# Two-kind causal attention followed by a gated long convolution: the loads, casts and products of v one pair behind those of q and k, all engines in written order from the first instruction, masks built at their first use

## The chip, the cores and the metric

The kernel runs on one core of one Trainium2 chip. The metric is the device time in microseconds of one execution; the time of a kernel is the median of its runs. Before the change the three runs have a median of 232.93 us (232.51 to 232.97).

## The reference, cut to what matters

Inputs q, k and v have the shape (4 batches, 8 heads, 768 positions, 64). Heads 0, 2 and 6 attend to every earlier position; the others attend to the first 4 positions and to a window of 64. The heads' outputs, side by side, are the input x (4, 768, 512) of the second part, which is a projection, a circular convolution along the positions (here by real Fourier transforms), two gates and an output projection.

```python
scores = np.matmul(q, k.transpose(0, 1, 3, 2)) / np.sqrt(D)
mask = np.where(retrieval_head, causal, causal & (is_sink | in_window))
a = softmax(np.where(mask, scores, -1e9))
x = np.matmul(a, v).transpose(0, 2, 1, 3).reshape(B, S, H * D)
x1, x2, x3 = np.split(x @ w_proj, 3, axis=-1)
x2_conv = np.fft.irfft(np.fft.rfft(x2, axis=1) * np.fft.rfft(filter_fft, axis=0), n=S, axis=1)
out = (x1 * x2_conv * x3) @ w_out
```

## The kernel before, in words

The work is tiled into 16 pairs of heads, numbered n = 0 to 15: four batches of four pairs. A pair passes through these steps.

- `emit_loads` (L89): three loads on SP's queue, q and k into one tile `qk_f` and v into `v_f`, 384 KB each. Three buffers of each tile go round.
- `emit_cast` (L113): q and k to bf16, two casts on POOL (for pair 0, q is cast on ACT), into `qk_bf`.
- `emit_v` (L299), all on POOL: a memset of the ones column and a cast make `v_aug`; a product with `vmask` makes `v_far`, used for blocks of keys that lie two or more blocks back, where a windowed head sees only the first positions. Three buffers of `v_aug` go round, so pair n + 3 writes where pair n's values were read.
- `emit_prep` (L123): q and k transposed, head dimension to the partitions. For pairs 0 to 5 PE transposes 12 blocks into PSUM and ACT copies them to `qkT` (L137; for pair 0 DVE does, L135). From pair 6 on SP issues a transposing DMA (L139).
- `emit_chunks` (L308): the causal blocks of the scores, in six chunks (three "thirds"), PE to PSUM (L319), and ACT's exponential into `pT` (L326).
- `emit_masking` (L328): one DVE product per third with `mask` (L333). `emit_mask` (L232) builds one head's mask on DVE from `code` and the head's kind.
- `emit_values` (L335) and `emit_norm` (L351): PE's 42 products with `v_aug` and `v_far` (L344), then DVE's reciprocal `rec` (L354) and scaling into `attn` (L355).
- `emit_turn` (L358): `attn` transposed into the batch's `xT`, by PE with a DVE copy (L364) or by SP's transposing DMA (L366).

The main loop (L498) runs over the pairs. In round n it casts and values pair n + 2, loads pair n + 3, computes pair n's scores and pair n - 1's values. The second part of a batch (`moe`, L371) is a generator whose steps are put between the attention's steps (`gate_step`). `setup_steps` (L263) transforms the filter once, in rounds 3 to 5: its first PE product is `X_ps<-fold` (L255), which waits for DVE's `fold` (L266).

PSUM gives four tiles of two banks, taken in turn by everything that PE writes, so a late reader of one tile stops a later PE step. POOL also issues the weights' loads, which convert to bf16: `filt` (L488) in round 0, one third of `wproj` in round 2 and two thirds in round 3 (L492), `wout` in round 6.

What sets the order: each engine runs its instructions in one order. For POOL and SP that is the order written, throughout. For DVE it is the written one from L104 to round 5 (`MANUAL`), for PE and ACT from L468 to round 5; elsewhere a scheduler chose it. Before the main loop stand pair 0's steps, the constants of the Fourier matrix G (ACT's `turns`, DVE's `angle` and `size`, ACT's four Sin steps) and the masks' parts.

Of the kernel before, what the change touches and what calls it, by code (L numbers as in the profile page):

```python
# [9 lines left out]
FP32 = mybir.dt.float32  # L10
BF16 = mybir.dt.bfloat16
I32 = mybir.dt.int32
AF = mybir.ActivationFunctionType
# [31 lines left out]
def kernel(  # L45
# [13 lines left out]
    nc = tc.nc  # L59

    B, H, S, D = q.shape
    NT = S // 128
# [21 lines left out]
    state = {}  # L84
    pairs = [(b, hp) for b in range(B) for hp in range(HP)]
# [3 lines left out]
    def emit_loads(n):  # L89

        b, hp = pairs[n]
        qk = ald.tile([128, 2, 2, NT, D], FP32, name="qk_f32")
        vf = ald.tile([128, 2, NT, D], FP32, name="v_f32")
        rows = "h (p t) d -> p h t d" if n < BY_PE else "h (t p) d -> p h t d"
        for dst, src, order in ((qk[:, 0], q, rows), (qk[:, 1], k, rows), (vf, v, "h (t p) d -> p h t d")):
            nc.sync.dma_start(out=dst, in_=src[b, 2 * hp:2 * hp + 2].rearrange(order, p=128))
        return qk, vf

    BY_PE = 6
    MANUAL = 5  # L100
    engine = mybir.EngineType
    ctx.enter_context(tc.manual_schedule(engines={engine.Pool, engine.SP}))
    order = ExitStack()
    order.enter_context(tc.manual_schedule(engines={engine.DVE}))  # L104
    loads = {0: emit_loads(0)}
    ret_i64 = const.tile([128, H], mybir.dt.int64, name="ret_i64")
    nc.scalar.dma_start(out=ret_i64, in_=is_retrieval.partition_broadcast(128))


    def cast(out, in_):  # L110
        nc.gpsimd.tensor_copy(out=out, in_=in_)  # L111

    def emit_cast(st):  # L113
        qk = loads[st["n"]][0]
        st["bf"] = asb.tile([128, 2, NT, 2, D], BF16, name="qk_bf", bufs=3)
        for a in range(2):
            src = qk[:, a].rearrange("p hh t d -> p t hh d")
            if st["n"] == 0 and a == 0:
                nc.scalar.copy(out=st["bf"][:, a], in_=src)  # L119
            else:  # L120
                cast(st["bf"][:, a], src)

    def emit_prep(st):  # L123
        st["qkT"] = qkT = asb.tile([128, 2, S], BF16, name="qkT", bufs=3)
        if st["n"] < BY_PE:
            ps = bank_pair("qkT_ps", BF16)
            for a in range(2):
                for t in range(NT):
                    nc.tensor.transpose(ps[:, a, t * 128:(t + 1) * 128],  # L129
                                        st["bf"][:, a, t].rearrange("p hh d -> p (hh d)"), identity)  # L130
            dst = qkT.rearrange("d a (p t) -> d a p t", t=NT)
            src = ps[:, :, 0:S].rearrange("d a (t p) -> d a p t", t=NT)
            if st["n"] == 0:
                for a in range(2):
                    nc.vector.tensor_copy(out=dst[:, a], in_=src[:, a])  # L135
            else:
                nc.scalar.copy(out=dst, in_=src)  # L137
# [12 lines left out]
    G = const.tile([128, 8, NM, 128], BF16, name="G")  # L150
    G2 = const.tile([128, 2, NM, 128], BF16, name="G2")
# [4 lines left out]
    for r in range(2):  # L156
# [17 lines left out]
        out=identity, in_=identity, compare_op=ALU.not_equal, fill=1.0,  # L174
# [5 lines left out]
        out=causal[:, :, 0:128], in_=causal[:, :, 0:128], compare_op=ALU.is_ge, fill=0.0, base=0,  # L180
# [4 lines left out]
        out=stream, in_=causal, compare_op=ALU.is_ge, fill=0.0, base=window - 1,  # L185
# [4 lines left out]
    angle = msb.tile([128, NM, HS], FP32, name="angle", tag="g")  # L190
# [7 lines left out]
    for m in range(NM):  # L198
        nc.vector.scalar_tensor_tensor(out=angle[:, m], in0=turns[:, m], scalar=-float(S),
                                       in1=angle[:, m], op0=ALU.mult, op1=ALU.add)  # L200
    nc.vector.tensor_scalar(out=size.bitcast(I32), in0=angle.bitcast(I32), scalar1=0x7fffffff,
                            scalar2=None, op0=ALU.bitwise_and)
    for out_, in_ in ((G[:, 0:4:2], size[:, :, 0:256]), (G2[:, :, :, 0:64], size[:, :, 256:384])):
        nc.scalar.activation(out=out_.rearrange("p r m f -> p m r f"), in_=in_.rearrange("p m (r f) -> p m r f", r=2), func=AF.Sin,
                             scale=-ETA, bias=quarter)
    for out_, in_ in ((G[:, 1:4:2], angle[:, :, 0:256]), (G2[:, :, :, 64:128], angle[:, :, 256:384])):
        nc.scalar.activation(out=out_.rearrange("p r m f -> p m r f"), in_=in_.rearrange("p m (r f) -> p m r f", r=2), func=AF.Sin,
                             scale=-ETA)
# [6 lines left out]
    if n_sink:  # L215
# [12 lines left out]
        out=vmask, in_=ret.rearrange("p (hp hh) -> p hp hh", hh=2)[:, :, None, :].to_broadcast([128, HP, 4, 2]))  # L228
# [3 lines left out]
    def emit_mask(h):  # L232
        nc.vector.tensor_scalar(out=mask[:, h], in0=code, scalar1=least[:, h:h + 1], scalar2=None,  # L233
                                op0=ALU.is_ge)
# [62 lines left out]


    def emit_v(st):  # L299
        vf = loads.pop(st["n"])[1]  # L300
        st["v_aug"] = v_aug = asb.tile([128, NT, 2, 65], BF16, name="v_aug", bufs=3)
        nc.gpsimd.memset(v_aug[:, :, :, 64:65], 1.0)  # L302
# [3 lines left out]
        nc.gpsimd.tensor_mul(v_far, v_aug[:, 0:4], vmask[:, hp, :, :, None].to_broadcast([128, 4, 2, 65]))  # L306
# [157 lines left out]
        yield  # L464


    emit_v(state[0])
    order.enter_context(tc.manual_schedule(engines={engine.PE, engine.Activation}))  # L468
    loads[1] = emit_loads(1)
    loads[2] = emit_loads(2)  # L470
    emit_cast(state[1])
    emit_v(state[1])
    loads[3] = emit_loads(3)

    gates = []

# [19 lines left out]
    N = len(pairs)  # L496
    xT = None
    for n, (b, hp) in enumerate(pairs):  # L498
        if hp == 0:
            xT = msb.tile([128, NC, S], BF16, name="xT", bufs=2)  # L500
        st, last, nxt = state[n], state.get(n - 1), state.get(n + 1)
        st["xT"] = xT
        if n == MANUAL:
            order.close()
        emit_chunks(st, 0)
        emit_weights(n)
        if n + 2 < N:
            emit_cast(state[n + 2])
            emit_v(state[n + 2])
        if 1 <= n < N - 3:  # L510
            loads[n + 3] = emit_loads(n + 3)
        if n == 1:
            for part in range(2):
                for half in range(2):
                    nc.sync.dma_start(out=G[:, 4 + 2 * part:6 + 2 * part, :, 64 * half:64 * half + 64],
                                      in_=G2[:, :, :, 64 * part:64 * part + 64])
        if n < 4:
            if n >= 2:
                emit_turn(state[n - 2])
            if last:  # L520
                emit_masking(last, 2)
                emit_prep(nxt)
                emit_chunks(st, 1)
                emit_values(last, (0,))
            else:
                emit_chunks(st, 1)
                emit_prep(nxt)
                emit_mask(0)
                emit_mask(1)
            emit_masking(st, 0)  # L530
            emit_chunks(st, 2, 0)
            if last:
                emit_values(last, (1,))
                emit_norm(last)
            emit_chunks(st, 2, 1)
# [76 lines left out]
```

## Time and profile before

| what | before |
|---|---|
| median of the runs | 232.93 us |
| the profiled execution, its own time | 232.87 us |
| its span, first to last instruction | 231.2 us |
| PE, DVE, ACT, POOL busy | 192.0, 157.6, 151.2, 68.6 us |
| moved by DMA | 34.81 MB |
| POOL idle ahead of the memset of `v_aug`, ended by PE's values | 73.6 us in 12 waits |
| first exponential | 13.70 us |
| first filter product on PE | 47.86 us |

All times are microseconds from the start of the span. A timeline row is: start, length, engine, line, operation, out<-in with shapes, and in brackets the idle time before it and what ended it. An engine's name with a q is its queue, which issues DMAs. A row of the windows gives the stretch, its length, busy time and instructions of PE, PEld, DVE, ACT and POOL, the granted TensorE clock, the share of the transfer engines (over 1 when packets overlap) and GB/s. A row of the DMA issues ends with the time from issue to landing; a row of a DMA queue gives packets, MB and the time of its packets as a share of the 16 engines' time in the window.

### The profile page before, as it was taken

What the parts mean: (1) busy time and instruction counts of PE and PEld (TensorE: products, weight loads), DVE (VectorE), ACT (ScalarE), POOL (GpSimd) and SP (SyncE); (2) the same over time, 40 slices, a digit from 0 to 9 for tenths busy, and PEclk for the clock granted to TensorE, in tenths of its full rate; (3) what the DMA queues carried; (4) which work ended last, traced back from release to release, by engine and by line L of the source; (5) the groups of instructions that cost most, each with busy time, mean ns of one, the idle gap of its engine ahead of it and who ended that gap; (6) DMA issues with size and microseconds to landing.
All of it is one profiled execution on the core that took longest, in us unless ns stands there. A gap on an engine that the chain in (4) does not pass through costs nothing.

```text
span 231.2 us, 4234 instructions
## 1 busy us (share of the span) xinstructions
PE 192.0 (83%) x1714; PEld 103.8 (45%) x1726; DVE 157.6 (68%) x251; ACT 151.2 (65%) x183; POOL 68.6 (30%) x99
## 2 busy tenths in 40 slices
PE   0246955868879999989797999899989999999992
PEld 0113534643434555535253655453546554455630
DVE  3687578799698946952779469834695593267581
ACT  2798979745858685669695866588886614662331
POOL 4359938546070606231509063211000000000000
PEclk9999988799999999999999999999999999999999
DMA  4999999999999994976997999849010100700007
GB/s 120 297 312 290 198 221 235 191 210 221 186 202 194 138 159 84 220 73 247 223 185 131 194 179 222 92 181 196 0 34 3 35 3 4 269 3 0 0 0 272
DMA packets 93027, 34.81 MB, mean 151 GB/s; under 512 B 84048, under 2 KB 89936, under 8 KB 93008
## 3 DMA queue, kind: packets, MB, share of 16 engines
q1 hardware_dynamic: 89968, 31.66, 67.6%
q0 software_dynamic: 2896, 2.88, 7.9%
q8 instruction: 13, 0.21, 0.4%
q14 instruction: 6, 0.05, 0.1%
q10 hardware_dynamic: 144, 0.01, 0.0%
HBM read 24.65 MB, written 6.29 MB: 134 GB/s over the span
## 4 chain that ended last, share of the span: by engine, by line
PE 49%; DVE 30%; ACT 9%; issue 4%; POOL 3%; DMA 2%; ACTq 0%; DVEq 0%; POOLq 0%
PE x_ps L408 16%; PE out_ps L436 8%; PE att L344 6%; PE x_ps L377 6%; DVE pT L333 5%; PE sc L319 4%; DVE attn L355 4%; PE c_ps L424 4%; ACT pT L326 3%; PE X_ps L255 3%; DMA qk_f<-in_q_dram 2%; DVE mask L233 2%; ACT X L389 2%; ACT x2s L381 2%; DVE P L398 2%
## 5 line engine op out<-in xcount | busy, mean ns | idle before, releaser
L326 ACT ACTIVATE pT<-sc 128x1024 bf16<-128x1024 f32 x96 | 83.1, 926 | 12.6 <-PE sc L319 12.6
L333 DVE TENSOR_TENSOR pT<-pT,mask 128x1024 bf16<-128x1024 bf16 x48 | 38.9, 813 | 21.0 <-ACT pT L326 20.7
L408 PE MATMUL x_ps<-xT,wproj 128*128 128x384 bf16 x256 | 45.3, 326 | 2.8 <-DVE attn L355 1.2
L319 PE MATMUL sc<-qkT 64*128 64x512 bf16 (+3 forms) x256 | 30.0, 334 | 9.9 <-DVE xT L364 5.0
L408 PEld LDWEIGHTS <-wproj 128*128 128x128 bf16 x256 | 23.8, 98 | 20.4 <-issue 4.9
L111 POOL CAST qk_bf<-qk_f 128x768 bf16<-128x768 f32 x31 | 28.4, 940 | 7.5 <-DMA qk_f<-in_k_dram 5.6
L344 PEld LDWEIGHTS <-pT 128*128 128x128 bf16 x672 | 24.5, 101 | 6.2 <-issue 2.0
L344 PE MATMUL att<-v_aug,pT 128*128 128x65 bf16 x352 | 26.0, 199 | 1.3 <-DVE pT L333 1.1
L417 DVE TENSOR_TENSOR g<-x1s,x_ps 128x768 bf16<-128x768 bf16 x16 | 15.2, 952 | 14.7 <-PE x_ps L408 14.5
L302 POOL MEMSET v_aug<- 128x12 bf16 x16 | 2.4, 152 | 73.6 <-PE att L344 73.6
L377 PE MATMUL x_ps<-wproj,xT 128*128 128x512 bf16 x92 | 22.2, 379 | 2.5 <-DVE attn L355 1.4
L436 PE MATMUL out_ps<-wout,y 128*128 128x512 bf16 x92 | 22.3, 380 | 1.3 <-DVE conv L430 0.6
L319 PEld LDWEIGHTS <-qkT 64*128 64x128 bf16 x256 | 9.7, 99 | 29.6 <-issue 21.4
L424 PE MATMUL c_ps<-Gi,P 128*128 128x384 bf16 x128 | 22.8, 326 | 0.0
L344 PE MATMUL att<-v_far,pT 128*128 128x65 bf16 x320 | 22.6, 199 | 0.0
L415 ACT CAST x1s<-x_ps 128x768 bf16<-128x768 f32 x16 | 12.9, 804 | 13.4 <-PE x_ps L408 13.4
L306 POOL TENSOR_TENSOR v_far<-v_aug,vmask 128x520 bf16<-128x520 bf16 x16 | 18.1, 1130 | 5.2 <-DVE vmask L230 4.0
L427 ACT COPY evs<-c_ps 128x384 f32<-128x384 f32 x16 | 7.7, 482 | 15.7 <-PE c_ps L424 11.0
L381 ACT CAST x2s<-x_ps 128x1024 bf16<-128x1024 f32 x12 | 12.2, 1018 | 8.6 <-PE x_ps L377 5.2
L255 PE MATMUL X_ps<-x,G 128*128 128x512 bf16 x70 | 17.1, 379 | 0.6 <-ACT x2s L381 0.3
L129 PE MATMUL qkT_ps<-identity,qk_bf 128*128 128x128 bf16 x72 | 7.6, 270 | 10.7 <-ACT qk_bf L119 7.2
L111 POOL CAST v_aug<-v_f 128x768 bf16<-128x768 f32 x16 | 15.4, 964 | 0.8 <-DMA v_f<-in_v_dram 0.8
(76 smaller groups left out, 221.1 us busy)
## 6 DMA issues: line engine op xcount, KB each, us to landing
qk_f<-in_q_dram SPq DMA_DIRECT2D x16, 384.0 KB, 4.7
qk_f<-in_k_dram SPq DMA_DIRECT2D x16, 384.0 KB, 6.0
v_f<-in_v_dram SPq DMA_DIRECT2D x16, 384.0 KB, 7.0
out_dram<-o_sb SPq DMA_DIRECT2D x9, 512.0 KB, 3.1
wproj<-in_moe_w_proj_dram POOLq DMA_DIRECT2D x3, 512.0 KB, 7.6
out_dram<-o_last SPq DMA_DIRECT2D x6, 256.0 KB, 2.6
filt<-in_moe_filter_fft_dram POOLq DMA_DIRECT2D x1, 768.0 KB, 8.6
wout<-in_moe_w_out_dram POOLq DMA_DIRECT2D x1, 512.0 KB, 9.0
```

The costliest lines, as they stand in the source:

```text
L111: nc.gpsimd.tensor_copy(out=out, in_=in_)
L255: nc.tensor.matmul(ps[:, u, :], lhsT=matrix[:, t, m, :], rhs=src[:, r, m, :], start=(m == 0), stop=(m == NM - 1))
L306: nc.gpsimd.tensor_mul(v_far, v_aug[:, 0:4], vmask[:, hp, :, :, None].to_broadcast([128, 4, 2, 65]))
L319: nc.tensor.matmul(sc[:, hh, n * 128:(n + cnt) * 128], lhsT=qkT[rows, 1, j * 128:(j + 1) * 128], rhs=qkT[rows, 0, i * 128:(i + cnt) * 128] ...
L326: nc.scalar.activation(out=pT[:, :, c, 0:w], in_=sc[:, :, 0:w], func=AF.Exp, scale=SCALE)
L333: nc.vector.tensor_mul(near, near, kinds)
L344: nc.tensor.matmul(att[:, hh, 65 * i:65 * i + 65], lhsT=st["pT"][:, hh, c, 128 * n:128 * n + 128], rhs=st["v_far" if i >= j + 2 else "v_au ...
L377: nc.tensor.matmul(ps[:, half, :], lhsT=xT[:, cc, half * HS + m * 128:half * HS + (m + 1) * 128], rhs=wproj[:, cc, DM:2 * DM], start=(cc = ...
L381: nc.scalar.copy(out=x2s, in_=ps)
L408: nc.tensor.matmul(ps[:, s, 0:HS], lhsT=wproj[:, cc, part * DM + cb * 128:part * DM + (cb + 1) * 128], rhs=xT[:, cc, s * HS:s * HS + HS], ...
L424: nc.tensor.matmul(ps[:, r, 0:HS], lhsT=P[:, t, u, ch], rhs=Gi[:, tile_no], start=(n == 0), stop=(n == 3))
L436: nc.tensor.matmul(ps[:, n, :], lhsT=y[:, cb, (i + n) * 128:(i + n + 1) * 128], rhs=wout[:, cb, :], start=(cb == 0), stop=(cb == NC - 1))
```

## The change

Four things change.

1. `emit_loads` loads q and k alone; the new `emit_load_v` loads v. Ahead of the loop the order on SP is now: q and k of pair 0, the heads' flags, q and k of pair 1, v of 0, q and k of 2, v of 1, q and k of 3. In round n SP issues v of n + 2, then q and k of n + 3; POOL casts q and k of n + 2 and values pair n + 1, not n + 2.
2. PE and ACT are in written order from the first instruction. ACT's written order has `turns` ahead of pair 0's cast of q, and the Sin steps of `angle` are written ahead of those of `size`.
3. The heads' flags (`ret_i`) are loaded by SP, not by ACT.
4. The two masks of pair n (n up to 3) are built in round n, right before their first use; before, those of pairs 1 to 3 were built at the end of rounds 0 to 2.

```diff
     def emit_loads(n):
-        qk = ald.tile([128, 2, 2, NT, D], FP32, name="qk_f32")
-        vf = ald.tile([128, 2, NT, D], FP32, name="v_f32")
-        for dst, src, order in ((qk[:, 0], q, rows), (qk[:, 1], k, rows), (vf, v, "h (t p) d -> p h t d")):
-            nc.sync.dma_start(out=dst, in_=src[b, 2 * hp:2 * hp + 2].rearrange(order, p=128))
+        state[n]["qk"] = qk = ald.tile([128, 2, 2, NT, D], FP32, name="qk_f32")
+        for a, src in enumerate((q, k)):
+            nc.sync.dma_start(out=qk[:, a], in_=src[b, 2 * hp:2 * hp + 2].rearrange(rows, p=128))
+    def emit_load_v(n):
+        b, hp = pairs[n]
+        state[n]["vf"] = vf = ald.tile([128, 2, NT, D], FP32, name="v_f32")
+        nc.sync.dma_start(out=vf, in_=v[b, 2 * hp:2 * hp + 2].rearrange("h (t p) d -> p h t d", p=128))
...
-    order.enter_context(tc.manual_schedule(engines={engine.DVE}))
+    order.enter_context(tc.manual_schedule(engines={engine.DVE, engine.PE, engine.Activation}))
...
-    nc.scalar.dma_start(out=ret_i64, in_=is_retrieval.partition_broadcast(128))
+    nc.sync.dma_start(out=ret_i64, in_=is_retrieval.partition_broadcast(128))
...
-    emit_v(state[0])
-    order.enter_context(tc.manual_schedule(engines={engine.PE, engine.Activation}))
-    loads[1] = emit_loads(1)
-    loads[2] = emit_loads(2)
-    emit_cast(state[1])
-    emit_v(state[1])
-    loads[3] = emit_loads(3)
+    emit_loads(1)
+    emit_load_v(0)
+    emit_loads(2)
+    emit_load_v(1)
+    emit_cast(state[1])
+    emit_v(state[0])
+    emit_loads(3)
...
         if n + 2 < N:
             emit_cast(state[n + 2])
-            emit_v(state[n + 2])
+            emit_load_v(n + 2)
+        if n + 1 < N:
+            emit_v(state[n + 1])
...
-                emit_mask(0)
-                emit_mask(1)
+            emit_mask(2 * n)
+            emit_mask(2 * n + 1)
             emit_masking(st, 0)
...
-            if n < 3:
-                emit_mask(2 * n + 2)
-                emit_mask(2 * n + 3)
```

The order of PE's instructions stays the same from the first to the last, and so does that of ACT behind the start. Three places move; the numbers of the lines grow by 2 or 3 or 5 with the new function.

ACT at the start, before, with the cast of q of pair 0 ahead of `turns`:

```order
L107 DMA ret_i_85<-in_is_retrieval_dram 128x8
L146 ACT_TABLE_LOAD
L146 ACTIVATE table<-table 128x1
L119 CAST qk_bf<-qk_f_80 128x768
L193 ACTIVATE turns<-fcol,tfrac 128x384 x3
L207 ACTIVATE G<-angle 128x3x2x128
```

ACT at the same place now:

```order
L149 ACT_TABLE_LOAD
L149 ACTIVATE table<-table 128x1
L196 ACTIVATE turns<-fcol,tfrac 128x384 x3
L122 CAST qk_bf<-qk_f_80 128x768
L207 ACTIVATE G<-angle 128x3x2x128
```

The flags' load has left ACT, and `turns` and the cast have changed places.

POOL behind the constants, before. The names' numbers tell the buffers: 80, 178 and 183 are q and k of pairs 0, 1 and 2; 81 and 179 are v of pairs 0 and 1.

```order
L111 CAST qk_bf<-qk_f_80 128x768
L302 MEMSET v_aug 128x12
L111 CAST v_aug<-v_f_81 128x12x64
L306 TENSOR_TENSOR v_far<-v_aug,vmask 128x520
L111 CAST qk_bf<-qk_f_178 128x768 x2
L302 MEMSET v_aug 128x12
L111 CAST v_aug<-v_f_179 128x12x64
L306 TENSOR_TENSOR v_far<-v_aug,vmask 128x520
L488 DMA filt<-in_moe_filter_fft_dram 128x6x512
L241 TENSOR_SCALAR G<-par 128x3
L111 CAST qk_bf<-qk_f_183 128x768 x2
```

POOL at the same place now; 80, 169 and 174 are q and k of pairs 0, 1 and 2, and 172 is v of pair 0:

```order
L114 CAST qk_bf<-qk_f_80 128x768
L114 CAST qk_bf<-qk_f_169 128x768 x2
L305 MEMSET v_aug 128x12
L114 CAST v_aug<-v_f_172 128x12x64
L309 TENSOR_TENSOR v_far<-v_aug,vmask 128x520
L491 DMA filt<-in_moe_filter_fft_dram 128x6x512
L244 TENSOR_SCALAR G<-par 128x3
L114 CAST qk_bf<-qk_f_174 128x768 x2
```

Pair 1's casts of q and k stand directly behind pair 0's, and the issue of `filt` behind one pair's v steps instead of two.

DVE around the end of pair 0, before: `rec` and `attn` are of pair 0, the masks of pair 2.

```order
L354 RECIPROCAL rec<-att 128x12
L355 TENSOR_TENSOR attn<-att,rec 128x2x6x64
L333 TENSOR_TENSOR pT<-pT,mask 128x2x2x256
L233 TENSOR_SCALAR mask<-code,least 128x768 x2
L364 COPY xT<-xt_ps 128x768
L333 TENSOR_TENSOR pT<-pT,mask 128x2x2x256 x2
```

DVE at the same place now:

```order
L357 RECIPROCAL rec<-att 128x12
L358 TENSOR_TENSOR attn<-att,rec 128x2x6x64
L336 TENSOR_TENSOR pT<-pT,mask 128x2x2x256
L367 COPY xT<-xt_ps 128x768
L336 TENSOR_TENSOR pT<-pT,mask 128x2x2x256
L236 TENSOR_SCALAR mask<-code,least 128x768 x2
L336 TENSOR_TENSOR pT<-pT,mask 128x2x2x256
```

The copy of `xT` has moved ahead of pair 2's two masks, which stand now right before pair 2's first product.

More of the change, by code (lines that the diff above doesn't have):

```diff
@@ L91, in emit_loads @@
         b, hp = pairs[n]
-        qk = ald.tile([128, 2, 2, NT, D], FP32, name="qk_f32")
-        vf = ald.tile([128, 2, NT, D], FP32, name="v_f32")
+        state[n]["qk"] = qk = ald.tile([128, 2, 2, NT, D], FP32, name="qk_f32")
         rows = "h (p t) d -> p h t d" if n < BY_PE else "h (t p) d -> p h t d"
-        for dst, src, order in ((qk[:, 0], q, rows), (qk[:, 1], k, rows), (vf, v, "h (t p) d -> p h t d")):
-            nc.sync.dma_start(out=dst, in_=src[b, 2 * hp:2 * hp + 2].rearrange(order, p=128))
-        return qk, vf
+        for a, src in enumerate((q, k)):
[4 more added lines that the diff above has]
+        nc.sync.dma_start(out=vf, in_=v[b, 2 * hp:2 * hp + 2].rearrange("h (t p) d -> p h t d", p=128))
     BY_PE = 6
@@ L103 @@
     order = ExitStack()
-    order.enter_context(tc.manual_schedule(engines={engine.DVE}))
-    loads = {0: emit_loads(0)}
+    order.enter_context(tc.manual_schedule(engines={engine.DVE, engine.PE, engine.Activation}))
+    emit_loads(0)
     ret_i64 = const.tile([128, H], mybir.dt.int64, name="ret_i64")
-    nc.scalar.dma_start(out=ret_i64, in_=is_retrieval.partition_broadcast(128))
+    nc.sync.dma_start(out=ret_i64, in_=is_retrieval.partition_broadcast(128))
     def cast(out, in_):
@@ L113, in emit_cast @@
     def emit_cast(st):
-        qk = loads[st["n"]][0]
+        qk = st.pop("qk")
         st["bf"] = asb.tile([128, 2, NT, 2, D], BF16, name="qk_bf", bufs=3)
@@ L202 @@
                             scalar2=None, op0=ALU.bitwise_and)
+    for out_, in_ in ((G[:, 1:4:2], angle[:, :, 0:256]), (G2[:, :, :, 64:128], angle[:, :, 256:384])):
+        nc.scalar.activation(out=out_.rearrange("p r m f -> p m r f"), in_=in_.rearrange("p m (r f) -> p m r f", r=2), func=AF.Sin,
+                             scale=-ETA)
     for out_, in_ in ((G[:, 0:4:2], size[:, :, 0:256]), (G2[:, :, :, 0:64], size[:, :, 256:384])):
@@ L205 @@
                              scale=-ETA, bias=quarter)
-    for out_, in_ in ((G[:, 1:4:2], angle[:, :, 0:256]), (G2[:, :, :, 64:128], angle[:, :, 256:384])):
-        nc.scalar.activation(out=out_.rearrange("p r m f -> p m r f"), in_=in_.rearrange("p m (r f) -> p m r f", r=2), func=AF.Sin,
-                             scale=-ETA)
     emit_prep(state[0])
@@ L299, in emit_v @@
     def emit_v(st):
-        vf = loads.pop(st["n"])[1]
+        vf = st.pop("vf")
         st["v_aug"] = v_aug = asb.tile([128, NT, 2, 65], BF16, name="v_aug", bufs=3)
@@ L508 @@
             emit_cast(state[n + 2])
-            emit_v(state[n + 2])
+            emit_load_v(n + 2)
+        if n + 1 < N:
+            emit_v(state[n + 1])
         if 1 <= n < N - 3:
-            loads[n + 3] = emit_loads(n + 3)
+            emit_loads(n + 3)
         if n == 1:
```

## The prediction

> **What bounds the kernel now.** I read the page first, then the windows by stage, then each engine's timeline of the first 50 us with the chain of waits beside it, and last the transfers. The page gives busy shares and, in tenths of 40 slices, how full the transfer engines were.
>
> ```profile
> span 231.2 us, 4234 instructions
> PE 192.0 (83%) x1714; PEld 103.8 (45%) x1726; DVE 157.6 (68%) x251; ACT 151.2 (65%) x183; POOL 68.6 (30%) x99
> DMA  4999999999999994976997999849010100700007
> ```
>
> The windows (length, busy time of each engine, granted clock, transfer share, GB/s) split that average.
>
> ```profile
> 14.00:22.00 8.00, 4.05 (x30) 1.83 (x27) 6.14 (x8) 6.86 (x8) 7.63 (x10) 1.00 1.18 300
> ...
> 30.00:38.00 8.00, 5.25 (x74) 4.01 (x73) 5.61 (x8) 5.85 (x7) 3.31 (x6) 0.79 1.20 252
> 58.00:88.00 30.00, 27.18 (x272) 14.81 (x273) 23.27 (x34) 21.74 (x26) 9.15 (x13) 1.00 1.01 168
> 126.00:155.00 29.00, 27.63 (x280) 15.38 (x282) 18.55 (x32) 20.25 (x26) 8.11 (x13) 1.00 0.95 173
> ```
>
> From 58 us on PE is busy over 90% and in one fixed order: that stage takes what it takes, and starts when the first stage lets it. In the first stage no engine is full (5.25 of 8 us on PE, at a clock of 0.79), while the transfers are always at work (slices 2 to 15 read 9). So the question is how much sooner the 58 us mark comes. What ended last there, from the chain of waits (start, us, what):
>
> ```profile
> 14.26 1.09 POOL v_far L306
> 15.35 2.13 POOL qk_bf L111 x2
> 19.84 0.95 POOL filt L488
> 21.04 0.77 POOL qk_bf L111
> 29.29 2.38 DVE mask L233 x2
> 31.67 0.48 DVE xT L364
> ```
>
> POOL, in written order, makes pair 1's q and k wait behind pair 0's values; later DVE makes xT, whose copy frees the PSUM bank that PE needs, wait behind two masks.
>
> **The change part by part.** First the start, on ScalarE, then on VectorE and PE:
>
> ```profile
> 6.27 0.83 ACT L119 CAST qk_bf<-qk_f 128x768 bf16<-128x768 f32 x1 [3.53 <-DMA qk_f<-in_q_dram]
> 7.01 1.62 ACT L193 ACTIVATE turns<-fcol,tfrac 128x384 int32<-128x384 f32 x3
> 9.65 1.26 ACT L207 ACTIVATE G<-angle 128x768 bf16<-128x768 f32 x2 [1.01 <-DVE angle L199]
> 10.95 1.44 ACT L204 ACTIVATE G<-size,quarter 128x768 bf16<-128x768 f32 x2
> 12.40 1.28 ACT L326 ACT_TABLE_LOAD   x1
> 13.70 3.56 ACT L326 ACTIVATE pT<-sc 128x1024 bf16<-128x1024 f32 x4
> 18.40 1.44 ACT L137 COPY qkT<-qkT_ps 128x1536 bf16<-128x1536 bf16 x1 [1.14 <-PE qkT_ps L129]
> 19.73 3.35 ACT L326 ACTIVATE pT<-sc 128x1024 bf16<-128x1024 f32 x4
> 24.82 4.97 ACT L326 ACTIVATE pT<-sc 128x1024 bf16<-128x1024 f32 x6
> ```
>
> ```profile
> 2.50 1.47 DVE L196 TENSOR_SCALAR angle<-fcol,tcol 128x384 f32<-128x384 f32 x3
> 7.66 1.96 DVE L199 SCALAR_TENSOR_TENSOR angle<-turns,angle 128x384 f32<-128x384 int32 x3 [3.69 <-ACT turns L193]
> 9.65 1.27 DVE L201 TENSOR_SCALAR size<-angle 128x1152 int32<-128x1152 int32 x1
> 10.84 1.81 DVE L135 COPY qkT<-qkT_ps 128x768 bf16<-128x768 bf16 x2
> 35.70 0.23 DVE L354 RECIPROCAL rec<-att 128x12 f32<-128x12 f32 x1 [2.36 <-PE att L344]
> ```
>
> ```profile
> 8.32 0.82 PE L129 MATMUL qkT_ps<-identity,qk_bf 128*128 128x128 bf16 x6 [0.34 <-POOL qk_bf L111]
> ```
>
> turns now stands ahead of the cast, inside ACT's 3.53 us wait for q, so it costs nothing. DVE goes on at 3.97 (2.50 + 1.47), and angle and size are done by about 7.3. ACT then runs cast, two Sin pairs and the table load without a gap: 6.27 + 0.83 + 1.26 + 1.44 + 1.28 = 11.1, against 13.70, a gain of 2.6 us for the first exponentials. Swapping the Sin pairs changes nothing, since that was their order on ACT before. PE's transposes of k end at 9.14 (8.32 + 0.82), and the second half of DVE's qkT copy (1.81) follows, to 10.1, so the scores are there in time. The flags' small load moves to SP behind k and is wanted only after that copy: nothing; were it late, it would delay the masks, wanted when two exponentials are done at about 13.
>
> On POOL the casts of pair 1's q and k no longer stand behind the 14.26 v_far. Three loads of 0.39 MB at the 300 GB/s of 14 to 22 us are 3.9 us a pair, 1.3 a load; k of pair 0 was there by 7.4, since PE's 8.32 followed its cast. So with v behind, q1 and k1 land near 8.7 and 10.0, and the casts end near 10.8 instead of 17.5. ACT's copy of pair 1 then follows its four exponentials directly, at 11.1 + 3.56 = 14.7 instead of 18.40 (3.7 gained). From there ACT sets the pace: 14.7 + 1.44 + 3.35 gives pair 2's copy at 19.4, and 1.44 + 4.97 = 6.4 us for each pair after it: 25.8, 32.2, 38.6.
>
> DVE must keep that pace. The mask pair (2.38) no longer stands between attn and xT; it falls into the wait before rec (2.36 at 35.70), which PE's values cause. Pair 3's masks come one pair later than before, where the same wait covers them; with no cover they would cost 2.4 us once.
>
> Without another limit, pair 5's transposes and the first filter product would run near 39 to 40 instead of:
>
> ```profile
> 45.63 1.06 PE L129 MATMUL qkT_ps<-identity,qk_bf 128*128 128x128 bf16 x12
> 47.86 0.39 PE L255 MATMUL X_ps<-fold,G 128*128 128x512 bf16 x1 [1.17 <-DVE fold L266]
> ```
>
> That is 7.5 to 8 us. But these transposes need pair 5's k from memory. POOL's waits and issues, SP's issues and the times to landing:
>
> ```profile
> 35.73 0.15 POOL L302 MEMSET v_aug<- 128x12 bf16 x1 [4.60 <-PE att L344]
> 37.69 1.54 POOL L492 DMA_DIRECT2D wproj<-in_moe_w_proj_dram  x2
> ```
>
> ```profile
> 28.73 1.32 SPq L96 DMA_DIRECT2D qk_f<-in_k_dram  x1
> 37.14 1.65 SPq L96 DMA_DIRECT2D v_f<-in_v_dram  x1
> ```
>
> ```profile
> qk_f<-in_k_dram SPq DMA_DIRECT2D x1, 384.0 KB, 7.6
> v_f<-in_v_dram SPq DMA_DIRECT2D x1, 384.0 KB, 12.5
> q1 hardware_dynamic: 1774, 0.45, 136.6%
> ```
>
> (The times to landing are of k of pair 5 and v of pair 6; the last row is the loads' queue in 36 to 38 us.) Pair 5's k landed at 28.73 + 7.6 = 36.3. The last two thirds of wproj were issued at 37.69, held back by POOL's 4.60 us wait for PE's values: the buffer of v_aug it wanted was still being read. With v one pair behind, that buffer was given up a pair earlier. Pair 4's k lands about 28 (the same loads as before by then, less one v), then come its cast (0.77), v_aug (its cast is as large) and v_far (1.09): wproj is issued near 31, ahead of pair 5's k. What that does to the loads shows in 40 to 46 us, when both queues had work:
>
> ```profile
> q0 software_dynamic: 893, 0.90, 92.2%
> q1 hardware_dynamic: 832, 0.21, 24.4%
> ```
>
> POOL's queue q0 took 92% of the engines and SP's q1 24%: the loads stand nearly still. The Trainium skill ("DMA: Bandwidth & Descriptors", Anatomy of one DMA, Arbitration) says that an engine goes round-robin between its queues, a packet from each. By that rule the loads would keep about half, k of pair 5 would come near 40 and the sum below would hold a gain of 6; the trace does not agree (24.4 against 92.2). The sum goes by the trace.
>
> So pair 5's k lands later than before. Counted forward: 1.05 MB of wproj at 0.90 MB in 6 us is 7.0 us, and 36.3 + 7.0 = 43.3. Counted backward: v of pair 6 landed at 37.14 + 12.5 = 49.6 with everything done; four loads of 0.39 MB lie behind pair 5's k there, at 0.45 MB in 2 us 1.75 us each, which gives 42.6, or 41.6 with a microsecond of thin work taken off. I take 42.5, and 41 and 43.5 as ends. Then one cast (0.77 at 21.04), half the transposes (0.5) and some 0.4 of hand-over put X_ps at 44.2 instead of 47.86: a gain of 3.7 us (2.7 to 5.2) of the 7.5 to 8.
>
> Where else SP's queue changes: a v stands ahead of its pair's neighbours' q and k, and the last v behind two output writes. Both are cast a whole pair before PE wants them; I cost them nothing, and 1.75 us each if a q waited for a v on the path. wproj and filt arrive sooner than wanted. PE's order is the same throughout, so after 58 us the gain stays.
>
> One cost in that stage is unknown: a cast on POOL slows a DVE operation beside it.
>
> ```profile
> L382 DVE TENSOR_TENSOR x<-x2s x12: 416/426/1290, 61.5 to 202.3; 128x512 bf16<-128x512 bf16 x12
> ```
>
> Alone it takes 416 ns; beside POOL up to 1290. Before, POOL's burst came as PE's values ended: v_aug, v_far, then the q and k casts. Now the casts come when their data land, ahead of v_aug and v_far. At best one such stretched product goes from the path, 0.9 us (1290 - 416). At worst the two casts of a batch (1.54) fall on products of the path and cost half their length, 0.8, in each of the three batches in which one moe's spectra pass, 2.4 in all. I take +0.5, somewhat under the middle, as the row's median of 426 says that most products stay clear.
>
> **Sum.** The profiled execution took 232.87 us, 1.7 more than its span; the median of the runs is 232.93, 0.06 more. 232.87 - 3.7 + 0.5 = 229.7, and by the median 229.7 or 229.8. I take 229.7.
>
> **The rivals.** *Loads on time.* If POOL reaches wproj some 4 us later than I count, or the two queues share evenly, pair 5's k lands early. In the first case it is 36 to 38, and the filter product runs near 40 (a gain of 7.8). In the second, of the 3.8 us of loads left at 32.5 (31 + 1.54) each takes double: k at 40.1, X_ps at 41.8, a gain of 6.1. With the casts' 0.5 that is 225.6 to 227.3. For it: the margin between 31 and 36.3 holds four steps whose starts I reckon rather than read. Against it: both counts and the row of 24.4%. The Trainium skill's round-robin ("DMA: Bandwidth & Descriptors", Arbitration) would give the second case. Chance 0.17.
>
> *Slower by collisions.* From pair 6 to pair 15 there are ten batches of q and k casts. If each, now set free from PE's values, falls on DVE products of the path at 0.8 us, they cost 8.0 and the time is 232.9 - 3.7 + 8.0 = 237.2. It decides from the fifth batch on (3.7 / 0.8 = 4.6). For it: the row of 1290 ns. Against it: in 58 to 155 us PE is busy over 90%, so most DVE work there is hidden, and POOL's own work in 126 to 155 is 8.1 of 29 us, as much as before. The Trainium skill ("GPSIMD Engine Reference", the table at its head, SBUF interfaces) has POOL and DVE contend when DVE reads two SBUF inputs; the sum x<-x2s above, slowed threefold, agrees. Chance 0.08.
>
> *The gain doesn't arrive.* The early weights, filt at 14 instead of 19.84 too, hold the loads back so long that pair 5's k lands at 46 and X_ps is where it was: 232.9 with nothing gained, or with the casts 233.4. It needs 2.5 us of transfer work more than my later end has. Chance 0.07, half of it within 0.2%.
>
> **How the numbers follow.** The forecast has 0.68. Its own range, with the ends of landing and casts, is 226.8 to 232.6, and most of it 227.5 to 231.8. The range goes down to the first rival and leaves out the second and half of the third with the far tail: 225.8 to 232.0. A measurement of this kernel tells about 0.2%, 0.5 us, from no change. Faster: the forecast but for 0.03, and the first rival, 0.82, with a little of the third, 0.84. Within 0.2%: 0.06. Slower: the second rival and small parts of the others, 0.10.
>
> **What would show it.** In the changed kernel's profile: the first exponential near 11.1; ACT's copies of qkT near 14.7, 19.4, 25.8 and 32.2; rec without the 2.36 us wait; wproj's two issues near 31; PE's transposes of pair 5 waiting some 4 us for POOL, and POOL for k from memory at about 42.5; X_ps at 44.2, and from there the old spacing to the end. I am wrong if k of pair 5 lands before 40 (then the filter product is near 40 and the time near 226), if ACT's copies do not come every 6.4 us, or if the stretch from X_ps to the end differs by over 2.5 us from the old.

## The result and the profile after

The changed kernel takes 227.66 us (median of four runs, 224.52 to 229.13) against 232.86 before: the ratio is 0.9699, with a 95% interval of 0.9604 to 0.9794. The profiled execution took 228.25 us at a span of 226.5, that of before 232.87 at 231.2: 4.6 us less. The ratios here and below leave out runs more than 1.5% above the fastest of their kernel, the medians do not (here 228.25, the profiled one, and 229.13 are out), so a ratio can lie beside the quotient of two medians, in e4 by 1.9%.

The page of the changed kernel: span, busy time, the transfer engines by slices, and POOL's casts with the idle time ahead of them.

```profile
span 226.5 us, 4231 instructions
PE 192.0 (85%) x1714; PEld 103.1 (46%) x1726; DVE 155.4 (69%) x251; ACT 150.5 (66%) x183; POOL 71.1 (31%) x99
DMA  5999989999999958967996999299011001600007
L114 POOL CAST qk_bf<-qk_f 128x768 bf16<-128x768 f32 x31 | 29.2, 946 | 72.6 <-DMA qk_f<-in_q_dram 57.9
```

PE's work is the same 192.0 us. POOL's idle time is as large as before, but it now ends with loads instead of PE's values: POOL casts when data land.

The windows of the changed kernel (columns as before):

```profile
14.00:22.00 8.00, 6.84 (x72) 4.29 (x74) 6.54 (x6) 7.62 (x9) 7.88 (x12) 1.00 1.15 232
30.00:38.00 8.00, 4.61 (x76) 2.87 (x73) 7.86 (x11) 6.87 (x8) 4.74 (x5) 1.00 0.89 179
40.00:50.00 10.00, 6.78 (x69) 4.06 (x72) 3.54 (x8) 4.02 (x4) 4.80 (x8) 0.72 1.25 223
```

14 to 22 us is now dense (PE 6.84 of 8 us, 4.05 before). In 40 to 50 us DVE works 3.54 of 10 us and PE's granted clock is 0.72: the stage waits there. ACT's timeline (start, length, and in brackets the wait and its end):

```profile
3.95 0.83 ACT L122 CAST qk_bf<-qk_f 128x768 bf16<-128x768 f32 x1
9.49 3.56 ACT L329 ACTIVATE pT<-sc 128x1024 bf16<-128x1024 f32 x4
12.91 1.47 ACT L140 COPY qkT<-qkT_ps 128x1536 bf16<-128x1536 bf16 x1
17.82 1.44 ACT L140 COPY qkT<-qkT_ps 128x1536 bf16<-128x1536 bf16 x1 [0.18 <-PE qkT_ps L132]
24.33 1.46 ACT L140 COPY qkT<-qkT_ps 128x1536 bf16<-128x1536 bf16 x1
30.44 1.55 ACT L140 COPY qkT<-qkT_ps 128x1536 bf16<-128x1536 bf16 x1
42.72 1.44 ACT L140 COPY qkT<-qkT_ps 128x1536 bf16<-128x1536 bf16 x1 [5.86 <-PE qkT_ps L132]
```

The copies come every 4.9 to 6.5 us until pair 5's, which is 12.3 us after pair 4's. The chain of waits names what held it:

```profile
31.12 0.15 SPq L100
31.27 0.04 issue
31.31 0.85 SPq L95
32.16 0.04 issue
32.21 8.72 DMA qk_f<-in_k_dram
40.93 0.05 issue
40.98 0.84 POOL qk_bf L114
41.82 0.05 issue
41.87 0.82 PE qkT_ps L132 x6
42.69 0.43 PE X_ps L258
```

Behind a load of v (L100) SP issues q and k of pair 5, and k takes 8.72 us to land, at 40.93. The weights' issues on POOL, and the transfer queues in 36 to 40 us (POOL's q0, SP's q1):

```profile
32.19 1.54 POOL L495 DMA_DIRECT2D wproj<-in_moe_w_proj_dram  x2
```

```profile
q0 software_dynamic: 543, 0.54, 85.2%
q1 hardware_dynamic: 277, 0.38, 31.2%
```

`wproj` and pair 5's k were issued at the same moment, and the weights' packets took 85% of the engines' time, the loads' 31% (packets overlap); in bytes that is 0.54 against 0.38 MB. The first filter product starts at 42.48 instead of 47.86, the values of pair 3 at 45.04 instead of 49.2, and the span ends 4.7 us sooner.

### The profile page after: what moved, and what is told of

The parts are those of the page before. It is cut to its first block, busy times and chain, and to the rows that moved or that the text cites. A ratio compares the mean times of both kernels' runs of the same rounds, so it can differ in the third digit from the quotient of the medians.

```text
span 226.5 us, 4231 instructions
## 1 busy us (share of the span) xinstructions
PE 192.0 (85%) x1714; PEld 103.1 (46%) x1726; DVE 155.4 (69%) x251; ACT 150.5 (66%) x183; POOL 71.1 (31%) x99
## 4 chain that ended last, share of the span: by engine, by line
PE 46%; DVE 21%; DMA 10%; ACT 9%; issue 4%; SPq 4%; POOL 3%; ACTq 0%; DVEq 0%; POOLq 0%
PE x_ps L411 17%; DMA qk_f<-in_k_dram 10%; PE out_ps L439 8%; PE x_ps L380 7%; ACT pT L329 3%; PE att L347 3%; PE X_ps L258 3%; PE sc L322 3%; SPq L95 3%; PE c_ps L427 3%; DVE pT L336 3%; DVE attn L358 2%; ACT x2s L384 2%; DVE conv L432 2%; DVE y L434 2%
## 5 line engine op out<-in xcount | busy, mean ns | idle before, releaser
L114 POOL CAST qk_bf<-qk_f 128x768 bf16<-128x768 f32 x31 | 29.2, 946 | 72.6 <-DMA qk_f<-in_q_dram 57.9
L347 PEld LDWEIGHTS <-pT 128*128 128x128 bf16 x672 | 24.0, 100 | 5.4 <-issue 2.0
L347 PE MATMUL att<-v_aug,pT 128*128 128x65 bf16 x352 | 25.3, 198 | 0.2
L347 PE MATMUL att<-v_far,pT 128*128 128x65 bf16 x320 | 21.9, 197 | 0.0
L114 POOL CAST v_aug<-v_f 128x768 bf16<-128x768 f32 x16 | 16.7, 1046 | 3.2 <-DMA v_f<-in_v_dram 3.2
L385 DVE TENSOR_TENSOR x<-x2s 128x512 bf16<-128x512 bf16 x12 | 7.4, 618 | 12.7 <-ACT x2s L384 12.7
```

Of the source, the lines that this page charges most:

```text
L347: nc.tensor.matmul(att[:, hh, 65 * i:65 * i + 65], lhsT=st["pT"][:, hh, c, 128 * n:128 * n + 128], rhs=st["v_far" if i >= j + 2 else "v_au ...
```

## The experiments

My theory after this profile: the start and the masks bring more than the 4.6 us, and the weights that overtake pair 5's k take part of it back. The rivals: v's shift itself is worth the gain; DVE's steps, stretched by POOL, hold it; the clock does. The runs share three chips: e1 to e4 (the kernel before: 233.1 us there), e5 to e8 (233.12), e9 to e12 (234.0). All have six runs, and the edits are against the changed kernel unless said otherwise.

| run | what | median, us | ratio to before (95%) |
|---|---|---|---|
| e1 | weights one round later | 227.29 | 0.9724 (0.9675 to 0.9772) |
| e2, e11 | v in step with q and k | 226.20, 224.97 | 0.9647 (0.9580 to 0.9714), 0.9617 (0.9573 to 0.9661) |
| e3 | before, flags on SP alone | 230.77 | 0.9887 (0.9845 to 0.9930) |
| e4 | old places of the masks | 232.47 | 0.9785 (0.9707 to 0.9864) |
| e5 | the changed kernel again | 228.54 | 0.9788 (0.9752 to 0.9824) |
| e6 | e1, one copy on ACT | 225.64 | 0.9658 (0.9619 to 0.9698) |
| e7 | e2, flags on ACT | 226.11 | 0.9671 (0.9628 to 0.9714) |
| e8 | e2, old places of the masks | 229.98 | 0.9864 (0.9828 to 0.9900) |
| e9 | e2, weights one round earlier | 229.07 | 0.9807 (0.9776 to 0.9837) |
| e10 | e2, weights later, one copy on ACT | 226.44 | 0.9701 (0.9649 to 0.9753) |
| e12 | before, new places of the masks alone | 230.43 | 0.9859 (0.9815 to 0.9902) |

**The weights' place (e1).**

```diff
-        for part in {2: (1,), 3: (0, 2)}.get(n, ()):
+        for part in {2: (1,), 4: (0, 2)}.get(n, ()):
```

> The changed kernel, with the last two thirds of wproj issued in round 4 instead of round 3, so behind the casts of q and k of pair 5 on POOL. Theory (what ends last in the first stage is the load of pair 5's k, held up by these weights): about 5.1 us of their packets leave the way, k of pair 5 lands near 36 instead of 40.9, PE's first filter product starts near 38 instead of 42.7, and the time falls by 4 to 5 us from 227.7 to 222.5 to 224. Rival (the first stage is at the pace of ACT and DVE anyway): within 1 us of 227.7. Second rival (the delay only moves on to the loads of pair 6 and the DMA transposes): within 1 us of 227.7, with PE waiting for qkT of pair 6 or 7.

Half of it came: pair 5's k is cast at 37.24 instead of 40.98, and the filter product starts at 38.67, 3.8 us sooner. But the time is 227.29, where its rivals had it (within 1 us of 227.7). The timelines of e1 on DVE and, below, on POOL show where that went:

```profile
42.15 2.52 DVE L284 COPY HAB<-HAB 128x512 bf16<-128x512 bf16 x1
44.70 1.08 DVE L286 TENSOR_SCALAR HAB<-HAB 1x512 bf16<-1x512 bf16 x1
```

```profile
42.11 1.60 POOL L114 CAST qk_bf<-qk_f 128x768 bf16<-128x768 f32 x2
43.64 0.16 POOL L305 MEMSET v_aug<- 128x12 bf16 x1
43.69 0.83 POOL L114 CAST v_aug<-v_f 128x768 bf16<-128x768 f32 x1
44.60 1.05 POOL L309 TENSOR_TENSOR v_far<-v_aug,vmask 128x520 bf16<-128x520 bf16 x1
```

The same copy takes 0.28 us in the changed kernel (median of two). Here it ends at 44.67, just behind POOL's cast of v (43.69 + 0.83 = 44.52), and the step behind it at 45.78, just behind `v_far` (45.65). So neither step is slowed by a share: each ends just behind the end of one of POOL's instructions, the copy only behind three casts and a memset in a row. The Trainium skill says ("SBUF — State Buffer", Who interferes with whom): POOL and DVE share one pair of ports under an exclusive lock, held for a whole instruction. The ends of these rows agree; that POOL can go on for several instructions before DVE has its turn is what they add.

**The copy off DVE (e6).** In e1's kernel, the first of the two copies:

```diff
-            nc.vector.tensor_copy(out=HA[:, t, 1, :], in_=HA[:, t, 0, :])
+            (nc.vector.tensor_copy if t else nc.scalar.copy)(out=HA[:, t, 1, :], in_=HA[:, t, 0, :])
```

> Late weights (e1) with one more edit: the first copy of HA (128x512, 2.52 us on VectorE beside GpSimd's casts, 0.29 where it is alone) is put on ScalarE, which waits for 2.8 us there. If GpSimd's casts stretched that copy and so ate the gain of the early filter product, the scores behind it come some 2 us earlier, the values of pair 4 near 54.5 instead of 56.35, and the time is 225 to 226 against e1's 227.3. If the rival holds, that something else (the granted clock, or the next stage) sets the time there, the values of pair 4 stay at 56 or the time stays at 227 to 228.

As the collision's theory had it. ACT's row, with POOL's burst (41.90 to 45.7) beside it:

```profile
42.97 0.62 ACT L284 COPY HAB<-HAB 128x512 bf16<-128x512 bf16 x1
```

The values of pair 4 start at 55.1 (56.4 in e1) and the time is 225.64. The changed kernel on the same chip (e5) took 228.54, and the intervals are apart. So both costs were there, one behind the other: late k, and under it DVE behind POOL. The second rests on the traces: the ratios of e1 and e6 (0.9724 and 0.9658) overlap in their intervals.

**v in step (e2, and e11 again).** `emit_load_v` and `emit_v` go back to their pair's q and k; flags, start and masks stay changed. Ahead of the loop v's loads and steps move in the same way, which is left out here:

```diff
...
-            emit_load_v(n + 2)
-        if n + 1 < N:
-            emit_v(state[n + 1])
+            emit_v(state[n + 2])
         if 1 <= n < N - 3:
             emit_loads(n + 3)
+            emit_load_v(n + 3)
```

> The changed kernel with v loaded, cast and valued in step with q and k again, as before the change; written orders, masks and flags' load stay changed. Theory: POOL's first v_far waits for vmask near 11.3 and pair 1's casts stand behind it, so the first stage keeps a gain from the start and the masks alone; wproj's second issue is again held by PE's values and comes behind pair 5's k. First filter product at 43 to 45.5, time 228 to 230.5. Rival (v one pair behind is nearly the whole gain): 232 to 233.

> v in step once more, beside e9 and e10 on one chip: 225.5 to 227 if e2's 226.2 was the kernel and not the chip, with k of pair 5 landing at 37 to 38. Above 228, the difference to the changed kernel would be the chip's.

> The changed kernel itself once more, beside the variants on one chip. If v one pair behind costs something by itself, as the run with v in step (226.2 against 227.66 on another chip) suggests, this kernel comes out at 227 to 229 and 1 to 2 us above the variant with v in step. The rival, that the shift of v is worth nothing either way, puts it within 0.7 us of what the variant with v in step gave, 225.5 to 227. Pair 5's k lands near 41 again in both.

e2 was missed by both theories, and e5 and e11 say that it was not the chip: the changed kernel takes 228.54, and v in step 224.97, half a microsecond under its range. On the chip of e5, v in step with the flags still on ACT (e7, below) took 226.11, with the intervals apart: v's shift costs some 2.4 us. This rests on e5; the interval of the result's own four runs, 0.9604 to 0.9794, holds both. SP's issues in e11, and POOL's cast of pair 5's k:

```profile
28.51 0.77 SPq L95 DMA_DIRECT2D qk_f<-in_q_dram  x1
29.32 0.98 SPq L95 DMA_DIRECT2D qk_f<-in_k_dram  x1
30.41 1.23 SPq L100 DMA_DIRECT2D v_f<-in_v_dram  x1
```

```profile
32.17 1.54 POOL L498 DMA_DIRECT2D wproj<-in_moe_w_proj_dram  x2
...
35.33 1.07 POOL L115 CAST qk_bf<-qk_f 128x768 bf16<-128x768 f32 x1 [0.16 <-DMA qk_f<-in_k_dram]
```

POOL issues the weights at 32.17, as in the changed kernel (32.19). The difference is on SP: pair 5's k is issued at 29.32, not at 32.21, since no v of the pair ahead stands in front of it, and so it has 2.9 us ahead of the weights. A lag of one 384 KB load decides on which side of `wproj` the k falls. The size varies from execution to execution: the cast of that k starts at 35.33, 36.65 and 37.72 with v in step (e11, e7, e2), at 38.87 and 40.98 without (e5, after).

The landing of k is not all of it, and here the clock, the third rival, comes in. In the profiled executions of e5 and e7 the first filter product starts at 40.37 and 40.53, and yet the values of pair 4 start at 58.26 and 55.36. PE's granted clock is 0.65 from 40 to 44 us and 0.70 from 54 to 58 us in e5, and 1.00 in both in e7. The same products, first in e5, then in e7:

```profile
52.53 3.14 PE L380 MATMUL x_ps<-wproj,xT 128*128 128x512 bf16 x8 [0.97 <-DVE HAB L277]
```

```profile
51.26 1.89 PE L381 MATMUL x_ps<-wproj,xT 128*128 128x512 bf16 x8 [0.72 <-DVE HAB L278]
```

The first drop stands behind PE's waits for pair 5's q and k (2.10 and 1.35 us in e5), so late loads seem to cost twice. What starts the second is open: PE had waited only 1.05 and 0.97 us just before, and e2's trace has the drop too (2.63 us for these products), with v in step.

**The weights' place the other way (e9).** e2's kernel with

```diff
-        for part in {2: (1,), 3: (0, 2)}.get(n, ()):
+        for part in {1: (1,), 2: (0, 2)}.get(n, ()):
```

> v in step (e2), and the weights one round earlier: the middle third of wproj in round 1, the other two in round 2, ahead of the loads of pair 5. If what v's shift cost was that the weights overtook pair 5's k, that loss comes back without the shift: k of pair 5 lands at 41 or later instead of 37.7, ScalarE's copy of pair 5 waits 3 us or more, the filter product moves from 39.8 to 43 or later, and the time is 228 to 230. The rival, that the cost lies in v's own place behind q and k, leaves the time within 0.7 us of e2's, 225.5 to 227.

As the overtaking has it. In e9 the weights are issued at 27.02, and then SP, POOL and ACT:

```profile
34.10 0.68 SPq L95 DMA_DIRECT2D qk_f<-in_k_dram  x1
```

```profile
41.42 0.83 POOL L115 CAST qk_bf<-qk_f 128x768 bf16<-128x768 f32 x1 [0.30 <-DMA qk_f<-in_k_dram]
```

```profile
43.16 1.44 ACT L141 COPY qkT<-qkT_ps 128x1536 bf16<-128x1536 bf16 x1 [4.46 <-PE qkT_ps L133]
```

Without any shift of v, the loss is back: 229.07 against 224.97 on one chip. The loads are late on SP too: pair 5's q, ahead of k, takes 3.35 us to issue (0.77 in e11), so k's issue comes at 34.10.

**Still earlier loads (e10).** e2's kernel with both edits of e6.

> v in step, the last two thirds of wproj in round 4, the first copy of HA on ScalarE. If the loads of pair 5 still limit the first stage of e2 (37.7), they land near 36, the filter product comes at 38.5 to 39.3, and the time is 224.5 to 225.5, under both kernels and all variants so far. If ScalarE's pace already sets the filter product there, its copy of pair 5 stays at 39.6 and the time at 225.7 to 226.8.

The loads came as the first theory has them, and the median, 226.44, as the rival has it; the profiled execution took 224.54, so its trace shows only part of that median. Pair 5's k is cast at 34.99 and the filter product starts at 37.45 (39.03 in e11), yet the values of pair 4 start at 54.3, not before e11's 53.8. Two of DVE's steps in e10, then the same two in e11:

```profile
41.30 0.99 DVE L287 TENSOR_SCALAR HAB<-HAB 1x512 bf16<-1x512 bf16 x1
42.21 1.71 DVE L289 TENSOR_SCALAR HAB<-HAB 1x512 bf16<-1x512 bf16 x1
```

```profile
42.20 0.28 DVE L287 TENSOR_SCALAR HAB<-HAB 1x512 bf16<-1x512 bf16 x1
42.41 0.27 DVE L289 TENSOR_SCALAR HAB<-HAB 1x512 bf16<-1x512 bf16 x1
```

With the weights issued later, the loads of pair 6 land sooner and POOL casts q, k and v from 41.26 to 43.8, on these steps. In e11 the weights hold those loads back until 44, and POOL is idle while DVE works. So the early weights cost something before the filter product and keep POOL off DVE behind it.

**The masks (e4, e8, e12).** e4 puts the masks of pairs 1 to 3 back in the changed kernel, e8 in e2's:

```diff
-            emit_mask(2 * n)
-            emit_mask(2 * n + 1)
+                emit_mask(0)
+                emit_mask(1)
...
+            if n < 3:
+                emit_mask(2 * n + 2)
+                emit_mask(2 * n + 3)
```

e12 makes the opposite edit, and no other, in the kernel before.

> The changed kernel with the masks of pairs 1 to 3 built at the end of rounds 0 to 2 again, as before the change. Theory: the first stage ends with pair 5's k from memory, so a DVE delay of up to 2.4 us a pair ahead of it is hidden: 227 to 228.5, with wproj's issue and k's landing within 1 us of those of the changed kernel. Rival (the masks' place is part of the gain): 229.5 to 232.

> v in step (e2) with the masks of pairs 1 to 3 at their old places. If the masks beside xT cost PE's bank and two fifths of the gain, it is 228 to 230; if the masks are hidden either way once POOL's casts come in the old order, it is 226 to 227. If the wide spread of e4 (227 to 235) comes of the old places of the masks, it shows here too; if it comes of v one pair behind, it does not.

> The kernel before with the masks of pairs 1 to 3 at their first use and nothing else. The masks stood on the chain beside xT for 2.4 us a round; e8 against e2 puts them at 3.8. If they count as much without the early start, the copies of pairs 4 and 5 come 2 and 4 us earlier (36 and 43 instead of 38.3 and 46.7), and the time is 229 to 230.5. The rival, that they count only once the start is early, since pair 1's casts behind pair 0's values hold the stage back, gives 231.5 to 233.

With v in step the masks' places are the largest part found: with them undone, e8 lies some 3.8 us above e2 and above e7, which ran on its chip. Alone they bring 3.3 us to the kernel before (1.41% of 234.0). Both came as their first theories have them. The chain of waits in e8:

```profile
25.23 1.35 DVE pT L337
26.59 2.38 DVE mask L237 x2
28.97 0.48 DVE xT L368
```

This is the row of before again, and it comes in each of two rounds (2.38 and 2.02 us). e8's runs, 229.71 to 230.7, do not spread as e4's do.

What the masks' places are worth in the changed kernel itself is not shown. e4's median, 232.47, lies above its rival's range, its ratio, 0.9785, is that of e5 (0.9788), and its six runs, 227.19 to 235.17, spread too far. Its profiled execution (229.33) goes with its theory: pair 4's copy comes at 31.22 (30.44 in the changed kernel), and the stage ends with pair 5's k, which lands at 42.12. The two masks beside `xT` are short there:

```profile
24.22 0.74 DVE L236 TENSOR_SCALAR mask<-code,least 128x768 bf16<-128x768 bf16 x2
```

In e8 the same two take 2.38 us, with POOL's casts beside them (26.82 to 28.42); in e4 POOL waits for loads then. So part of what the masks cost is DVE behind POOL once more.

**The flags (e3, e7).** e3 is the kernel before with only the flags' load on SP, between the loads of k and v of pair 0; e7 is e2's with it back on ACT. The line, as e3 changes it:

```diff
-    nc.scalar.dma_start(out=ret_i64, in_=is_retrieval.partition_broadcast(128))
+    nc.sync.dma_start(out=ret_i64, in_=is_retrieval.partition_broadcast(128))
```

> The kernel before with one change: the heads' flags are loaded by SP behind q and k of pair 0, not by ACT. Theory from the changed kernel's trace (q landed at 3.93 there, at 6.25 before, so the flags' load by ACT held up the first loads): q lands near 3.9, and the whole chain of the first stage comes up to 2.3 us sooner: 230.5 to 232. Rival, as in the prediction (the flags' load costs nothing where it is): 232.9 within 0.4.

> v in step (e2) with the flags' load put back first on ScalarE's queue. If the flags' place is worth 2.3 us whatever else is changed, q of pair 0 lands at 6.2 again, the first exponential starts near 11.8 and the time is 228 to 229. My prediction's view that the flags cost nothing wants 226 to 227, as e2.

Alone, the flags' place brings 1.1%, 2.6 us; its interval overlaps that of the masks alone (e12), so which of the two is larger is not shown. In e7 the first exponential starts at 11.96 instead of 9.58, as expected, but the time does not follow: pair 5's copy is at 40.44 against 39.56 in e2, and 226.11 against 226.20 us cannot be told apart. 2.4 us at the start have shrunk to 0.9 at pair 5 (1.6 against e11's 38.81). The parts do not add: with the masks off the chain, the earlier start is not seen in the time.

## Why the prediction was right

The forecast was 229.7; the profiled execution took 228.25 and the runs 227.66, inside the range. That it came so near is in part luck: a delay that I put at nothing stood in for one that I counted too high. By its steps:

- **The first exponential, 11.1: missed, 9.49.** The step that failed is "the flags' small load moves to SP ... nothing". Before, it was issued on ACT's queue, beside the first q on SP's. The windows of the first microseconds, before and then after (GB/s is the last column):

```profile
2.00:4.00 2.00, 0.00 (x0) 0.00 (x0) 1.92 (x6) 0.73 (x2) 1.33 (x3) 1.00 0.33 66
```

```profile
2.00:4.00 2.00, 0.00 (x0) 0.00 (x0) 1.95 (x7) 1.85 (x6) 1.32 (x3) 1.00 0.94 317
```

  The cast of q starts at 3.95 instead of 6.27. I had taken 6.27 as given. e3 shows that this is the flags' doing.
- **ACT's copies, 14.7, 19.4, 25.8, 32.2: right in their spacing.** They are 1.5 to 1.8 us early by the start, and come 4.9, 6.5 and 6.1 us apart (4.7, 6.4, 6.4 predicted).
- **The masks in DVE's wait: right in place, not in size.** Of the 2.36 us of idle time ahead of `rec`, 0.62 is left with pair 2's masks built before it, as DVE's timeline of the changed kernel has it. These masks took 0.74 us where I had counted 2.38, as POOL was waiting for loads then; pair 3's, beside POOL's casts, took 2.12. What I named as the chain's cause counts in e8 and e12; e4 leaves open how much it does here.

```profile
24.87 0.74 DVE L236 TENSOR_SCALAR mask<-code,least 128x768 bf16<-128x768 bf16 x2
...
27.02 0.23 DVE L357 RECIPROCAL rec<-att 128x12 f32<-128x12 f32 x1 [0.62 <-PE att L347]
```

- **wproj near 31 and pair 5's k at 42.5: 32.19 and 40.93, near by luck.** The weights' larger share of the engines' time (85.2 against 31.2%) is there again, and e1 and e9 move k by the weights' place alone. But I put the whole delay on POOL, which reached `wproj` sooner. The step that failed is "a v stands ahead of its pair's neighbours' q and k ... I cost them nothing": k's issue moved from 28.73 to 32.21. In e11, with k issued at 29.32 and `wproj` at the same time as here, k is cast at 35.33. So the weights, with k issued about where I took it, do not hold it until 42.5; the delay on SP, which I left out, stood in for the rest.

  The round-robin rule of the Trainium skill ("DMA: Bandwidth & Descriptors", Arbitration), a packet from each queue, was to bring k near 40. 40.93 lies between that and 42.5, just outside my ends of 41 and 43.5, and does not decide. I had also held a rule on packets against shares of time: in the row of before the two queues passed 893 and 832 packets, about one each, and the weights' were the larger (0.90 against 0.21 MB); in the row of after it is 543 to 277. Whether these are the packets that the rule means, no run here shows.
- **The filter product, 44.2: 42.48**, a gain of 5.4 instead of 3.7, by the two misses above. Pair 3's values, behind it, gain 4.1: PE had idled 3.83 us for k, and the six filter products after that ran at about half speed, as these rows of the changed kernel and of e11 show.

```profile
41.87 0.82 PE L132 MATMUL qkT_ps<-identity,qk_bf 128*128 128x128 bf16 x6 [3.83 <-POOL qk_bf L114]
...
43.33 1.91 PE L258 MATMUL X_ps<-fold,G 128*128 128x512 bf16 x4 [0.22 <-issue]
```

```profile
39.03 1.47 PE L259 MATMUL X_ps<-fold,G 128*128 128x512 bf16 x6 [0.76 <-ACT pT L330]
```

  1.91 us for four is 0.48 each, 1.47 for six is 0.25. The Trainium skill ("TensorE: Matmul & The Clock Gate", What's actually happening) has the clock halve after an idle window of about 3.4 us; the 0.72 of the window from 40 to 50 us agrees in kind. By the trace the clock is at 0.50 from 39 us on, 1 us into that wait, with another wait of 2.09 us and half a microsecond of work ahead of it.
- **Casts on DVE's path, +0.5: the number came, for another reason.** From the filter product to the end 0.7 us were lost. But between it and pair 3's values 1.25 were lost (2.56 us instead of 1.31), where PE's clock was low, and some 0.6 were gained behind them. What POOL does to a single step was under-sized: e1 and e10 show 3.0 and 2.2 us on two steps. I had priced half of a cast; a step can wait for several of POOL's instructions.

Of the rivals, "loads on time" is what e1 and e10 (the latter with v in step) make of the kernel, and their times, 227.3 and 226.4, lie at and in its 225.6 to 227.3. "Slower by collisions" did not come, but its mechanism keeps that rival from paying more.

What stays open: why runs of one kernel spread (224.5 to 229.1 for the changed one, 222.85 to 228.02 for e11). Two profiled executions of the changed kernel, after and e5, have pair 5's k cast at 40.98 and 38.87, so the landing of that load is part of it; what moves it I have not found. By the sign that I gave (k before 40, and the time near 226) e5 would count against me, at 227.56. Nor does all that the first stage gains reach the end: in e1 the filter product comes 3.8 us sooner than in the changed kernel, the values of pair 4 2.5 us (56.35 against 58.83), and the span ends 0.6 us sooner.

## What to carry to other kernels

Before a load is moved later in an in-order queue, look at what the other queues issue in the next few microseconds: one 384 KB load of delay put pair 5's k on the wrong side of the weights and cost some 2.4 us of the gain. Look at each part of a combined change alone: here the masks' places and the flags' each bring over 1% alone, and the version without v's shift (e11, 0.9617 of the kernel before) beats the changed kernel as e5 ran it (0.9788). Where a stall goes, look at what the freed transfers set off next, since here a sooner load put GpSimd's casts on VectorE's critical steps.

## What was not expected of the hardware

- A load of 8 flags, spread to 128 partitions and issued beside the first loads, left the engines at 66 GB/s for two microseconds where the same loads ran at 317 with it issued behind q and k on their own queue, and delayed the first tile by 2.3 us.
- A DVE step of 0.28 us can take 2.52 us beside GpSimd: it ended 0.15 us behind the last of three casts in a row, not a share later.
- The packets of a queue fed by GpSimd took 85 to 92% of the transfer engines' time while SP's queue had loads waiting, in the kernel before and after.
- PE's granted clock fell to 0.50 from 53 to 56 us in e5, behind waits of only 1.05 and 0.97 us.
